# Turning attention outputs by two half-height row groups of TensorE: a sliding-window attention and mixture-of-experts kernel

## The chip, the cores and the metric

The kernel runs on one core of a Trainium2 chip as one program. The metric is the device time of one execution in microseconds (us), lower is better; a run's time is compared with the kernel before on the same chip. Engines are named as in the profile: PE is TensorE (PEld its weight loads), DVE is VectorE, ACT is ScalarE, POOL is GpSimd, SP issues transfers.

## The reference

Attention with a window of 64 positions runs over 8 batches of 8 heads, 576 positions and 64 values each. Its output, laid out as 4608 tokens by 512 values, is x. Each token goes to the one of 8 experts with the largest logit, and its result is scaled by that expert's softmax weight.

```python
rel = pos[:, None] - pos[None, :]
mask = (rel >= 0) & (rel < window)
scores = np.where(mask, scores, -1000000000.0)
scores = scores - np.max(scores, axis=-1, keepdims=True)
attn = np.exp(scores)
attn = attn / (np.sum(attn, axis=-1, keepdims=True) + 1e-09)
x = (attn @ v).transpose(0, 2, 1, 3).reshape(B * S, H * D)
logits = x @ w_gate
expert_idx = np.argmax(logits, axis=1)
probs = np.exp(logits - logits.max(-1, keepdims=True))
probs /= probs.sum(-1, keepdims=True) + 1e-09
gate_w = probs[np.arange(N), expert_idx]
y = np.maximum(x_e @ w1[e], 0.0) @ w2[e]        # for the tokens of each expert e
out = gate_w[:, None] * y
```

## The kernel before, in words

The program has two parts. In the first, attention and routing run in one software pipeline of 48 steps; in the second, the tokens of each expert are gathered and go through the two expert products. The change touches the first part alone.

A unit is two batches (a batch group) and two heads, and there are 16 units, four to a batch group. A unit has three steps; a step handles three tiles of 128 query positions for both heads. The function step (L1089) writes out, for a step s, what each engine does in order, and every engine runs its own list in that order:

- scored(s + 1) (L743): 24 products of q and k into banks 0 and 1 of PSUM, one bank per head; masked(s + 1) (L756) on DVE adds the mask and takes the row minimum; softened (L766) on ACT takes the exponentials.
- weighted(s - 1) (L791): 24 products with v into bank 6.
- logits (L846), in the third step of a unit only: 18 products with the gate's weights for the unit before; L851 or L853 on DVE adds them up.
- flipped(s) (L775): 12 transposes of the exponentials, each over 64 partitions, six into one bank and six into another. L778 copies the first bank to SBUF on DVE (pT, first half) and the second on ACT (second half).
- divided(s - 1) (L801, L802, L805) on DVE reads bank 6 and writes x into the tile xs.
- turned(s + 3): transposes of q and k, L707 (16 of 64 partitions, two banks, two copies L713 on ACT) or, in the third step of a unit, L698 (two of 128 partitions, one bank, copy L701).
- x_turned(s - 2) (L818): three transposes of x over 128 partitions into one bank, and the copy L821 on ACT into a tile xT, which the logits read later.

The banks of flipped, turned, x_turned and logits come from one ring, tr_ring (L594): banks 2, 3, 4, 5 and 7 in turn. A use of a bank waits until the use five places earlier has been copied out. From step 41 on the ring has four banks (L1139).

Three names for steps are used below. x_turned(s - 2) handles the third of a unit's three parts in a **middle step** (s mod 3 = 1), the first part in a **closing step** (s mod 3 = 2, the one with the logits and L698), and the second part in a **pair step** (s mod 3 = 0).

Of the kernel before, what the change touches and what calls it, by code (L numbers as in the profile page):

```python
# [11 lines left out]
F32 = mybir.dt.float32  # L12
# [24 lines left out]
def kernel(  # L37
# [10 lines left out]
    nc = tc.nc  # L48
    P = nc.NUM_PARTITIONS
    B, H, S, D = q.shape  # L50
# [39 lines left out]
    ident = consts.tile([P, P], F32, name="ident")  # L90
# [38 lines left out]
    banks = [Memory(banks_p.tile([P, 512], F32, name=f"bank{i}")) for i in range(8)]  # L129
# [54 lines left out]
    with tc.tile_pool(name="tmp", bufs=1) as tmp:  # L184
# [8 lines left out]
        for i in range(BG):  # L193
# [14 lines left out]
            out=behind[:], in_=behind[:], pattern=[[-1, P]], compare_op=ALU.is_ge, fill=0.0, base=0,  # L208
# [44 lines left out]
    ST = 3  # L253
    NST = NTB // ST
# [331 lines left out]
    with tc.manual_schedule(), ExitStack() as brief, ExitStack() as held:  # L586
# [2 lines left out]
        rp = held.enter_context(tc.tile_pool(name="rp", bufs=2))  # L589
        att = brief.enter_context(tc.tile_pool(name="att", bufs=2))  # L590
        sd = brief.enter_context(tc.tile_pool(name="sd", bufs=3))
        xp = brief.enter_context(tc.tile_pool(name="xp", bufs=3))
        lt = brief.enter_context(tc.tile_pool(name="lt", bufs=1))
        sc_ring, tr_ring = cycle((0, 1)), cycle((2, 3, 4, 5, 7))  # L594

# [6 lines left out]
            out=half[:, n : n + 1], in_=half[:, n : n + 1], fill=MASKED, pattern=[[0, 1], [rest[0], P]],  # L602
# [16 lines left out]
        units = [(bg, g) for bg in range(B // BG) for g in range(NG)]  # L619
        NU = len(units)  # L620

        halves = (slice(0, D), slice(D, P))
        qks, sides, rests, Ts, xss, xTs, lgs, logits_of = {}, {}, {}, {}, {}, {}, {}, {}
# [185 lines left out]

        last = B // BG - 1  # L810

        def x_turned(s):
            u, c = divmod(s, NST)
            bg, g = units[u]
            xTs[s] = xp.tile([P, ST * P], F32, name="xT")
            tr = banks[next(tr_ring)](0, ST, P)
            for m in range(ST):
                nc.tensor.transpose(  # L818
                    out=tr[:, m, :], in_=xss[bg, c][:, m, g * P : (g + 1) * P], identity=ident[:]
                )  # L820
            nc.scalar.copy(out=xTs[s][:], in_=tr.rearrange("p m s -> p (m s)"))  # L821
# [267 lines left out]
        def step(s):  # L1089
# [30 lines left out]
            if 0 <= s - 2 < N:  # L1120
                x_turned(s - 2)
# [15 lines left out]
        for s in range(-3, N):  # L1137
            if s == N - NST * NG + NST + 2:
                tr_ring = cycle((2, 3, 4, 5))  # L1139
# [6 lines left out]
        tr_ring = cycle((4, 5))  # L1146
# [6 lines left out]
        for c in (1, 2):  # L1153
            store(last, c, nc.sync)
        x_turned(N - 2)
        sums_x(tps)
        gather_first(perm_e[:, C : 2 * C])
        by_tok = [by_tokens(last, c) for c in range(NST)]
        next(by_tok[0])
        next(tile0)  # L1160
        logit(N - 2)
        x_turned(N - 1)
        next(by_tok[0], None)
        next(by_tok[1])
# [167 lines left out]
```

## Time and profile before

| | |
|---|---|
| median of 3 runs | 688.19 us (686.51 to 688.44) |
| the profiled execution's own time | 684.57 us |
| its span | 682.8 us |
| PE busy over the span | 656.1 us (96%) |
| ACT busy over the span | 284.3 us (42%) |
| DVE busy over the span | 494.2 us (72%) |

The span runs from the first to the last instruction that the profiler saw. A row of the timeline has the start, the busy length, the engine, the line, the operation and what it writes and reads, and how many instructions were merged into it; in square brackets stands how long the engine was idle before and what released it. Matmuls overlap, so a group's busy length reaches into the next group's: what a group costs PE is the time from its start to the next group's start.

### The profile page before, as it was taken

What the parts mean: (1) busy time and instruction counts of PE and PEld (TensorE: products, weight loads), DVE (VectorE), ACT (ScalarE), POOL (GpSimd) and SP (SyncE); (2) the same over time, 40 slices, a digit from 0 to 9 for tenths busy, and PEclk for the clock granted to TensorE, in tenths of its full rate; (3) what the DMA queues carried; (4) which work ended last, traced back from release to release, by engine and by line L of the source; (5) the groups of instructions that cost most, each with busy time, mean ns of one, the idle gap of its engine ahead of it and who ended that gap; (6) DMA issues with size and microseconds to landing.
All of it is one profiled execution on the core that took longest, in us unless ns stands there. A gap on an engine that the chain in (4) does not pass through costs nothing. (4 is left out here: it accounts for less than half of the span.)

```text
span 682.8 us, 18995 instructions
## 1 busy us (share of the span) xinstructions
PE 656.1 (96%) x7385; PEld 571.5 (84%) x7385; DVE 494.2 (72%) x1598; ACT 284.3 (42%) x699; POOL 354.5 (52%) x407
## 2 busy tenths in 40 slices
PE   7799999999889999999999999999999999999996
PEld 4678878787779987988999999899699789699995
DVE  5678998998839666856686676577775786866864
ACT  5779898999833222212222212212331222232220
POOL 7556777573171337578451546546285566264112
PEclk9999999999999999999999999999999999999999
DMA  9999979684360461725501280270254171212021
GB/s 205 233 268 305 208 197 275 172 245 135 129 203 6 146 227 55 248 64 172 191 12 54 65 276 34 79 265 32 67 191 161 47 270 46 65 41 65 4 62 63
DMA packets 94657, 95.22 MB, mean 139 GB/s; under 512 B 58063, under 2 KB 73439, under 8 KB 94528
## 3 DMA queue, kind: packets, MB, share of 16 engines
q1 hardware_dynamic: 72000, 34.58, 19.8%
q10 hardware_dynamic: 13920, 32.05, 13.7%
q0 software_dynamic: 8608, 26.88, 12.5%
q8 instruction: 80, 1.31, 0.8%
q14 instruction: 49, 0.40, 0.2%
HBM read 74.32 MB, written 20.74 MB: 139 GB/s over the span
## 5 line engine op out<-in xcount | busy, mean ns | idle before, releaser
L337 DVE STREAM_TRANSPOSE v_m<-xg 32x256 f32<-32x256 f32 x320 | 139.3, 435 | 19.5 <-ACT xg L322 13.4
L293 POOL DMA_INDIRECT xg<-x_dram,at_g x42 | 44.5, 1059 | 171.7 <-ACT qk_m L349 122.5
L366 PE MATMUL bank<-qk_m,s 128*128 128x128 f32 x1024 | 122.5, 275 | 0.0
L366 PEld LDWEIGHTS bank<-qk_m,s 128*128 128x128 f32 x1024 | 118.3, 192 | 0.1
L766 ACT ACTIVATE pr<-pr,mx 128x128 f32<-128x128 f32 x288 | 89.7, 396 | 12.9 <-DVE mx L756 12.7
L366 PE MATMUL bank<-qk_m,w 128*128 128x128 f32 x768 | 94.1, 276 | 0.6 <-PEq L1236 0.6
L366 PEld LDWEIGHTS bank<-qk_m,w 128*128 128x128 f32 x768 | 90.4, 192 | 4.0 <-issue 3.6
L756 DVE CUSTOM_DVE_ANT_0 pr<-bank,mask 128x128 f32<-128x128 f32 x288 | 64.5, 285 | 19.7 <-PE bank L743 18.2
L408 DVE TENSOR_TENSOR v_m<-bank,v_m 128x256 f32<-128x256 f32 (+1 forms) x95 | 43.9, 480 | 35.5 <-PE bank L412 26.6
L312 POOL DMA_INDIRECT out_dram<-v_m,at_s x42 | 42.6, 1013 | 50.8 <-DVE v_m L408 46.9
L791 PEld LDWEIGHTS bank<-v_m,pT 128*64 128x64 f32 x1152 | 40.6, 139 | 14.6 <-DVE xs L805 9.6
L146 POOL TENSOR_TENSOR s<-w 128x1024 f32<-128x1024 f32 x22 | 52.2, 2375 | 0.0
L791 PE MATMUL bank<-v_m,pT 128*64 128x65 f32 x1152 | 47.3, 229 | 4.6 <-DVE xs L805 2.7
L412 PE MATMUL bank<-qkT_m,v_m 128*128 128x256 f32 x216 | 48.1, 379 | 0.0
L679 POOL COPY v_m<-v_m 64x520 f32<-64x520 f32 x32 | 20.1, 628 | 51.8 <-DMA v_m<-in_v_dram 41.3
L349 ACT COPY qk_m<-v_m 128x512 f32<-128x512 f32 x40 | 22.7, 615 | 57.0 <-DVE v_m L337 57.0
L412 PEld LDWEIGHTS bank<-qkT_m,v_m 128*128 128x128 f32 x216 | 41.0, 190 | 5.6
L373 ACT COPY qk_m<-bank 128x512 f32<-128x512 f32 x16 | 9.4, 586 | 86.3 <-PE bank L366 66.4
L743 PE MATMUL bank<-qkT_m 64*64 64x128 f32 x1152 | 44.2, 282 | 0.4 <-DVE mx L756 0.3
L378 DVE TENSOR_TENSOR qk_m<-bank,qk_m 128x512 f32<-128x512 f32 x16 | 11.1, 692 | 38.4 <-PE bank L366 24.1
L743 PEld LDWEIGHTS bank<-qkT_m 64*64 64x64 f32 x1152 | 32.1, 134 | 8.0 <-issue 3.4
L412 PE MATMUL bank<-s,v_m 128*128 128x256 f32 x168 | 37.4, 379 | 0.0
(212 smaller groups left out, 1234.7 us busy)
## 6 DMA issues: line engine op xcount, KB each, us to landing
w<-in_moe_w_dram ACTq DMA_DIRECT2D x11, 2048.0 KB, 8.2
qk_m<-in_q_dram SPq DMA_DIRECT2D x32, 256.0 KB, 5.0
v_m<-in_v_dram SPq DMA_DIRECT2D x64, 128.0 KB, 4.6
qk_m<-in_k_dram SPq DMA_DIRECT2D x30, 256.0 KB, 5.1
qk_m<-in_moe_w_dram ACTq DMA_DIRECT2D x3, 2048.0 KB, 10.7
w<-in_moe_w_dram ACTq DMA_DIRECT2D x4, 512.0 KB, 5.6
x_dram<-xs POOLq DMA_DIRECT2D x4, 512.0 KB, 4.9
x_dram<-xs SPq DMA_DIRECT2D x4, 512.0 KB, 5.4
```

The source lines that it names most:

```text
L146: op()
L293: G.indirect_dma_start(out=xg_all[:, c], out_offset=None, in_=x_dram[:, :], in_offset=bass.IndirectOffsetOnAxis(ap=at_g[:, c : c + 1], axi ...
L312: put = G.indirect_dma_start(out=out[:, :], out_offset=bass.IndirectOffsetOnAxis(ap=at_s[:, c : c + 1], axis=0), in_=ys[c], in_offset=None ...
L337: V.transpose(out=xn[b * QD : (b + 1) * QD, :, :, a * QD : (a + 1) * QD], in_=rows[a * QD : (a + 1) * QD, :, :, b, :],)
L349: nc.scalar.copy(out=xq[:, :, c], in_=xn[:, c])
L366: nc.tensor.matmul(acc[:, f, :], lhsT=a[:, g, f * P : (f + 1) * P], rhs=b[:, g, :], start=(first and f == 0 and g == 0), stop=(g == HG - 1 ...
L408: plus = lambda out, a, b: V.tensor_tensor(out=out, in0=a, in1=b, op=ALU.add)
L412: nc.tensor.matmul(acc, lhsT=a[:, f, :], rhs=b[:, f, :], start=(start and f == 0), stop=(stop and f == HF - 1), skip_group_check=True,)
L743: nc.tensor.matmul(out_, lhsT=qT[rows, t, a * WINDOW : (a + 1) * WINDOW], rhs=rhs, start=True, stop=True, skip_group_check=True,)
L756: V.tensor_tensor_reduce(out=prs[h][:, m, :], in0=scs[h][:, m, :], in1=mask[:, m0 + m, :], scale=-scale, scalar=-2 * MASKED, op0=ALU.add, ...
L766: nc.scalar.activation(out=y, in_=y, func=AF.Exp, scale=-1.0, bias=mx[:, h, m : m + 1])
L791: nc.tensor.matmul(px[a * D : (a + 1) * D, h, m, :], lhsT=pTs[a][:, h, m, :], rhs=vt[:, h, :], start=True, stop=True, skip_group_check=True,)
```

## The change

The x of the first two parts of a unit is turned together, in the pair step, for all units but the last; the closing step turns no x. Each 128x128 transpose is replaced by two of 64 partitions, one over partitions 0 to 63 and one over 64 to 127, which write to two banks. Twelve such transposes stand where three of 128 partitions stood, and two copies on ACT, one per bank, each 128x384 in pieces of 64, stand where one stood. The third part is turned as before. The xT tiles are split into a pool of two and a pool of one double tile.

```diff
-        xp = brief.enter_context(tc.tile_pool(name="xp", bufs=3))
+        xp = brief.enter_context(tc.tile_pool(name="xp", bufs=2))
+        xp2 = brief.enter_context(tc.tile_pool(name="xp2", bufs=1))
...
+        def x_pair(u):
+
+            bg, g = units[u]
+            xT = xp2.tile([P, 2, ST, P], F32, name="xT2")
+            trs = [banks[next(tr_ring)](0, 2, ST, D) for _ in range(2)]
+            for c in range(2):
+                xTs[u * NST + c] = xT[:, c].rearrange("p m s -> p (m s)")
+                for m in range(ST):
+                    for tr, r in zip(trs, halves):
+                        nc.tensor.transpose(
+                            out=tr[:, c, m, :], in_=xss[bg, c][r, m, g * P : (g + 1) * P], identity=ident[r, r]
+                        )
+            for tr, r in zip(trs, halves):
+                nc.scalar.copy(
+                    out=xT.rearrange("p c m s -> p (c m) s")[:, :, r], in_=tr.rearrange("p c m s -> p (c m) s")
+                )
+
         def x_turned(s):
             u, c = divmod(s, NST)
             bg, g = units[u]
+            if u < NU - 1 and c < 2:
+                if c == 1:
+                    x_pair(u)
+                return
             xTs[s] = xp.tile([P, ST * P], F32, name="xT")
```

In the changed kernel the line numbers shift: L743, L775, L707 and L698 become L744, L776, L708 and L699, the transposes of x_pair are L822, and the matmuls of the routing at L901 become L923. In the rows below bank_81 to bank_88 are banks 0 to 7, in order, and a name such as side_1914 is one buffer of the tile side. DVE_49 and Activation_49 stand for a semaphore that the engine raises.

The first place is PE's list in a pair step of the middle of the program, from flipped to the next scored. Before:

```order
L775 MATMUL bank_84<-ident,pr_1848 128x64
L775 MATMUL bank_85<-ident,pr_1848 128x64
...
L707 MATMUL bank_86<-ident,side_1821 128x64 [waits Activation_49,Pool_49]
L707 MATMUL bank_88<-ident,side_1821 128x64 [waits Activation_49]
...
L818 MATMUL bank_83<-ident,xs 128x128 [waits Activation_49]
L818 MATMUL bank_83<-ident,xs 128x128 x2
L743 MATMUL bank_81<-qkT_m 64x128 [waits DVE_49]
```

And in the changed kernel:

```order
L776 MATMUL bank_83<-ident,pr_1876 128x64
L776 MATMUL bank_84<-ident,pr_1876 128x64
...
L708 MATMUL bank_85<-ident,side_1849 128x64 [waits Pool_49]
L708 MATMUL bank_86<-ident,side_1849 128x64 [waits Activation_49]
...
L822 MATMUL bank_88<-ident,xs 128x64 [waits Activation_49]
L822 MATMUL bank_83<-ident,xs 128x64 [waits DVE_49]
...
L744 MATMUL bank_81<-qkT_m 64x128
```

The step took five banks of the ring and now takes six, so the second bank of x_pair (83) is the one that flipped wrote first in the same step, and its transposes wait for DVE, whose L778 copies that bank out.

The second place is PE's list in step 41, a closing step, where the ring has just become four banks long; L901 is the routing's product of an earlier batch group. Before:

```order
L775 MATMUL bank_83<-ident,pr_3978 128x64
L775 MATMUL bank_84<-ident,pr_3978 128x64
...
L698 MATMUL bank_85<-ident,qk_m 128x128 x2
L818 MATMUL bank_86<-ident,xs 128x128 x3
L901 LDWEIGHTS behind [waits DVE_49]
L901 MATMUL bank_83<-oh_all,behind 128x72 [waits Activation_49]
L743 MATMUL bank_81<-qkT_m 64x128 [waits DVE_49]
```

And in the changed kernel:

```order
L776 MATMUL bank_83<-ident,pr_4046 128x64
L776 MATMUL bank_84<-ident,pr_4046 128x64
...
L699 MATMUL bank_85<-ident,qk_m 128x128 x2
L923 LDWEIGHTS behind
L923 MATMUL bank_86<-oh_all,behind 128x72 [waits DVE_49]
L744 MATMUL bank_81<-qkT_m 64x128 [waits DVE_49]
```

The three transposes of x are gone from the closing step, as in every closing step up to step 44, and L923 has the fourth bank (86) where it had the first (83), so it no longer waits for ACT.

The third place is PE's list in the next step, 42, a pair step with four banks. Before:

```order
L707 MATMUL bank_86<-ident,side_4048 128x64 [waits Activation_49,Pool_49]
L707 MATMUL bank_83<-ident,side_4048 128x64 [waits Activation_49]
...
L818 MATMUL bank_84<-ident,xs 128x128 [waits DVE_49]
L818 MATMUL bank_84<-ident,xs 128x128 x2
L743 MATMUL bank_81<-qkT_m 64x128
```

And in the changed kernel:

```order
L708 MATMUL bank_85<-ident,side_4116 128x64 [waits Activation_49,Pool_49]
L708 MATMUL bank_86<-ident,side_4116 128x64 [waits Activation_49]
...
L822 MATMUL bank_83<-ident,xs 128x64 [waits DVE_49]
L822 MATMUL bank_84<-ident,xs 128x64 [waits Activation_49]
...
L744 MATMUL bank_81<-qkT_m 64x128
```

Here the first bank of x_pair waits for DVE's copy of the same step, as the one bank did before, and the second waits for ACT's.

## Rows read from the trace of the kernel before

**Rows 1.** Timeline of PE over one unit, closing step to closing step (us).
```profile
100.98 0.59 PE L775 MATMUL bank<-ident,pr 64*128 64x64 f32 x12
101.50 0.44 PE L698 MATMUL bank<-ident,qk_m 128*128 128x128 f32 x2
101.78 0.49 PE L818 MATMUL bank<-ident,xs 128*128 128x128 f32 x3
102.20 0.89 PE L743 MATMUL bank<-qkT_m 64*64 64x128 f32 x24
103.18 0.97 PE L791 MATMUL bank<-v_m,pT 128*64 128x65 f32 x24
104.08 0.58 PE L775 MATMUL bank<-ident,pr 64*128 64x64 f32 x12
104.50 0.67 PE L707 MATMUL bank<-ident,side 64*128 64x64 f32 x16
105.10 0.55 PE L818 MATMUL bank<-ident,xs 128*128 128x128 f32 x3
105.57 0.89 PE L743 MATMUL bank<-qkT_m 64*64 64x128 f32 x24
...
109.60 0.97 PE L791 MATMUL bank<-v_m,pT 128*64 128x65 f32 x24
...
111.29 0.58 PE L775 MATMUL bank<-ident,pr 64*128 64x64 f32 x12
```

**Rows 2.** The same unit, DVE.
```profile
101.11 0.55 DVE L853 TENSOR_TENSOR lgT<-bank,lgT 96x384 f32<-96x384 f32 x1 [0.33 <-PE bank L846]
...
102.56 0.56 DVE L805 TENSOR_TENSOR xs<-bank,rec 128x384 f32<-128x384 f32 x1
104.69 0.56 DVE L778 COPY pT<-bank 128x384 f32<-128x384 f32 x1 [0.21 <-PE bank L775]
```

**Rows 3.** The same unit, ACT.
```profile
106.61 0.48 ACT L821 COPY xT<-bank 128x384 f32<-128x384 f32 x1
106.98 1.88 ACT L766 ACTIVATE pr<-pr,mx 128x128 f32<-128x128 f32 x6
108.75 0.48 ACT L778 COPY pT<-bank 128x384 f32<-128x384 f32 x1
```

**Rows 4.** Waits of PE from 20 to 195 us: total, times, longest.
```profile
PE bank L707 <- POOL side L652: 4.1, 3, 2.5
PE bank L791 <- DVE xs L805: 2.7, 9, 0.5
```

**Rows 5.** Timeline of PE and ACT in two units with routing work.
```profile
88.70 0.97 PE L791 MATMUL bank<-v_m,pT 128*64 128x65 f32 x24 [0.47 <-DVE xs L805]
98.76 0.47 ACT L778 COPY pT<-bank 128x384 f32<-128x384 f32 x1
99.13 1.07 PE L791 MATMUL bank<-v_m,pT 128*64 128x65 f32 x24
```

**Rows 6.** Timeline of steps 41 and 42, PE, DVE and ACT.
```profile
167.54 0.20 PE L901 MATMUL bank<-oh_all,behind 128*128 128x72 bf16 x1 [0.49 <-ACT pT L778]
167.71 0.89 PE L743 MATMUL bank<-qkT_m 64*64 64x128 f32 x24
168.65 0.29 DVE L756 CUSTOM_DVE_ANT_0 pr<-bank,mask 128x128 f32<-128x128 f32 x1 [1.21 <-PE bank L743]
170.73 0.55 PE L818 MATMUL bank<-ident,xs 128*128 128x128 f32 x3 [0.21 <-DVE pT L778]
170.81 0.46 ACT L778 COPY pT<-bank 128x384 f32<-128x384 f32 x1
171.21 0.89 PE L743 MATMUL bank<-qkT_m 64*64 64x128 f32 x24
```

**Rows 7.** Timeline of step 44, a closing step, and what follows it.
```profile
179.36 0.89 PE L743 MATMUL bank<-qkT_m 64*64 64x128 f32 x24
180.40 0.29 DVE L756 CUSTOM_DVE_ANT_0 pr<-bank,mask 128x128 f32<-128x128 f32 x1 [0.53 <-PE bank L743]
```

## The prediction

> **What bounds the kernel now.** I read the page first (PE busy in nearly every slice), then PE's timeline over one undisturbed unit, DVE's and ACT's beside it, the table of waits, and last the steps in which PE stands still. The change lives in the first 190 us; the expert part behind it has the same instructions and simply starts earlier or later.
>
> In the undisturbed unit [rows 1] PE is hardly ever idle: from 104.08 to 111.29 each group starts when the one before is through. A unit takes 111.29 - 100.98 = 10.31 us. One stop is left, in the closing step. There L791 starts at 103.18 because bank 6 is being read by L805 on DVE until 102.56 + 0.56 = 103.12 [rows 2]; the release takes 0.06. DVE itself is late because its list goes L853, L778, L801, L802, L805, and L853 waits for PE's logits [rows 2]. So a closing step is a chain from the logits on PE through DVE back to PE, and x is no part of it. PE waits for L805 nine times in the table [rows 4].
>
> **Prices.** On PE, from start to start [rows 1]:
> - twelve transposes of 64 partitions, followed by another such group: 104.08 to 104.50, 0.42;
> - twelve followed by a group of another shape: 100.98 to 101.50, 0.52; so a change of shape costs 0.10;
> - sixteen and a change: 104.50 to 105.10, 0.60; without the change 0.50;
> - three of 128 partitions and a change: 0.42 in the closing step, 0.47 in the pair step; without the change 0.32.
>
> **Closing step: x removed.** L743 starts 0.32 earlier, at 101.88. L791 behind it still starts at 103.18, for L805 is unmoved: DVE's list hangs on the logits, which come before. L756 follows L805 on DVE and is unmoved too. Gain on the path: nothing, hidden by L805. ACT does one copy less, 0.37 from start to start (106.61 to 106.98 is one copy's share [rows 3]); its exponentials then wait for L756 anyway.
>
> **Pair step: x of two parts.** Without any wait, sixteen of L707 with no change of shape behind them (0.50) and twelve of x_pair with one (0.52) are 1.02, where 104.50 to 105.57 was 1.07: L743 would start 0.05 earlier. But the order shows that the second bank of x_pair is the bank that flipped wrote first in the same step, and waits for L778 on DVE. That copy runs from 104.69 to 105.25 [rows 2], since it waits for the twelve transposes of flipped itself; with 0.06 for the release the second transpose starts at 105.31. The first one has gone ahead at 105.00 and gains nothing: PE's list is served in order, so the other ten, L743, L791, and in time the logits stand behind the blocked one. From 105.31 the pairs and the change of shape take 0.47 to 0.52 (the twelve's price, with or without its first pair): L743 at 105.78 to 105.83, against 105.57. I take +0.2, near the lower one.
>
> Nothing takes this back before the closing step, since PE has no gap up to 111.29; logits, L853 and L805 move by 0.2, and so does the next unit. The 0.32 saved there is hidden as above. An undisturbed unit becomes 10.31 + 0.2 = 10.51.
>
> ACT now does two x copies in the pair step, so its exponentials start at 107.35 instead of 106.98 and the copy of pT behind them ends at 108.75 + 0.48 + 0.37 = 109.60 [rows 3]. L791 needs it at 109.60 [rows 1], and with PE 0.2 late at 109.80: covered, by PE's own delay alone. If that cover were gone it would cost about 0.06 here. In a unit where it is thin already the whole 0.37 counts: L791 at 99.13 reads pT, whose copy ends at 98.76 + 0.47 = 99.23 [rows 5]. Writing in pieces of 64 instead of a whole row is not in the trace; the copy is bounded by 0.37, its share, and 0.48, its full length, and I take 0.37, the price of the row that it replaces.
>
> The single double tile xT2 costs nothing: the logits that read it run in the closing step before the next pair step. No transfer is added or moved on SP's or POOL's queue.
>
> [...] Here the step goes from five banks of a five-bank ring to six, and rows of this trace show what a ring too short costs: in step 42, with four banks, L818 stood 0.21 for DVE's copy of the same step [rows 6].
>
> **The last steps, with four banks.** In step 41 L901 loses its wait of 0.49 for ACT [rows 6] (another bank), and with 0.32 of x gone L743 starts some 0.8 earlier; L756 has waited 1.21 for it, so DVE follows, and ACT as far as its own list lets it, about 0.6 with one copy less. In step 42 x_pair's second bank waits for ACT's copy of pT, which ended at 170.81 + 0.46 = 171.27; 0.6 earlier plus 0.06 and 0.47 gives L743 at 171.20, where it was 171.21. So PE gives its gain back there, while DVE and ACT keep theirs: between 0 and -0.6, I take -0.3. In step 44, a closing step, L805 does not bind; L756 waited 0.53 for L743 [rows 7], so the 0.32 of x is a real gain, -0.3. In step 45 nothing of q and k is turned and the banks are free; the same chain runs on to the gather that opens the second part.
>
> **Sum.** There are 15 pairs. The first two fall before PE's stops for POOL's sorted q and k (4.1 us in three stops [rows 4]), which swallow 0.2: 0. One falls in a unit whose middle step waits 0.47 for DVE's routing work before L791 at 88.70 [rows 5]: 0. Ten stand in units like the one above: nine at 0.2 and the one at 99.13 with 0.4 make +2.2. The last two: -0.6. Together +1.6: 684.57 becomes 686.2 in the profiled execution (span 682.8 and some 1.8 around it). That execution is 3.6 below the median of the runs, 688.19; the difference put on the median gives 689.8.
>
> **Rivals.**
> 1. The saved PE time reaches the end, because DVE's copies come early enough or the chain through L805 yields. Then a unit saves 0.05 + 0.32 = 0.37, twelve units 4.4, with the tail 5.0: 683.2. For it: PE is busy throughout. Against: L791 at 103.18 ends on L805 to within the release time, and in the pair step the copy ends 0.25 after the first transpose is free to go. [...]
> 2. ACT becomes the bound, place: exponentials and pT of the middle step, price 0.37 a unit, decisive where the copy of pT ends less than 0.37 before L791 needs it. Twelve units 4.4, less 0.6: +3.8, 692.0. For it: the unit at 99.13. Against: in the undisturbed unit PE is late by more than ACT lags, and the closing step gives ACT its copy back.
> 3. The wait is there, but routing work on DVE or ACT hides it in most units, as at 88.70: ten units at 0 to 0.1, with the tail -0.6 to +0.4: about 688. That the halves are not turned together at all would change little by itself: the first half then goes ahead alone, which is what the wait makes of the first pair.
>
> **How the numbers follow.** Forecast 0.52, rival 1 0.15, rival 2 0.13, rival 3 0.20. About 0.3%, or 2.1 us, is what a measurement of this kernel tells from no change. The forecast's own range, 0.1 to 0.3 a unit and the tail between 0 and -0.9, is 688.3 to 691.2; it is on the slower side of the bound four times in ten. Slower: 0.20 of the forecast, 0.12 of rival 2 and 0.01 of rival 3, 0.33. Faster: 0.13 of rival 1 and 0.01 of rival 3, 0.14. Same: 0.53. The range takes in rival 3 and reaches to rival 2 and towards rival 1: 685.6 to 692.2.
>
> **What would show it.** In an undisturbed pair step the transposes of x_pair should show a stop of some 0.3 ended by DVE's pT, and L743 should start 1.27 after the start of the q and k transposes instead of 1.07; in the closing step L743 should be earlier and L791 not, with a longer stop for L805; the unit should be 10.5. Step 41's L923 should show no stop. A unit of 10.0 would make the closing step's reasoning wrong, one of 10.7 the cover of ACT.

## The result: slower, and most of it behind the attention

The changed kernel takes 695.75 us (693.72 to 696.22) against 687.7 of the kernel before; the ratio is 1.0113, with a 95% interval of 1.0087 to 1.0139. I had forecast 689.8 with a range up to 692.2. The profiled execution has a span of 694.5 us against 682.8.

The attention does nearly what was predicted. PE's timeline over an undisturbed ("clean") unit (start, duration, operation, and in brackets the idle time before it with what ended it); it answers to [rows 1]:

```profile
102.55 0.59 PE L776 MATMUL bank<-ident,pr 64*128 64x64 f32 x12
...
103.44 0.89 PE L744 MATMUL bank<-qkT_m 64*64 64x128 f32 x24
104.75 0.97 PE L792 MATMUL bank<-v_m,pT 128*64 128x65 f32 x24 [0.42 <-DVE xs L806]
105.65 0.59 PE L776 MATMUL bank<-ident,pr 64*128 64x64 f32 x12
106.07 0.67 PE L708 MATMUL bank<-ident,side 64*128 64x64 f32 x16
106.58 0.22 PE L822 MATMUL bank<-ident,xs 64*128 64x64 f32 x1
106.95 0.59 PE L822 MATMUL bank<-ident,xs 64*128 64x64 f32 x11 [0.15 <-DVE pT L779]
107.47 0.89 PE L744 MATMUL bank<-qkT_m 64*64 64x128 f32 x24
...
113.18 0.52 PE L776 MATMUL bank<-ident,pr 64*128 64x64 f32 x10
```

One transpose of x_pair goes ahead at 106.58, the other eleven wait for DVE's copy of pT until 106.95, and the closing step's saved time ends in a stop of 0.42 for L806 (the lines have moved by one: L805 is L806, L778 is L779). The unit takes 113.18 - 102.55 = 10.63 instead of 10.31. DVE's copy, which answers to the last of [rows 2], and PE's waits from 20 to 197 us (total, times, longest), which answer to [rows 4]:

```profile
106.34 0.56 DVE L779 COPY pT<-bank 128x384 f32<-128x384 f32 x1 [0.39 <-ACT pr L767]
```

```profile
PE bank L792 <- DVE xs L806: 6.7, 17, 0.7
...
PE bank L822 <- DVE pT L779: 2.9, 13, 0.7
...
PEld bank L792 <- ACT pT L779: 0.4, 2, 0.2
```

At the last L791 of the attention the changed kernel is 2.1 us behind, at 200 us 5.3, and it stays at 4.9 to 5.3 until 590 us. Then comes something that the prediction does not have. PE's timeline in the expert part of the changed kernel, and the same matmuls in the kernel before:

```profile
594.92 0.63 PE L519 MATMUL bank<-w,qk_m 128*32 128x256 f32 x6
598.54 5.85 PE L519 MATMUL bank<-w,qk_m 128*32 128x256 f32 x36 [2.99 <-issue]
```

```profile
589.96 5.52 PE L519 MATMUL bank<-w,qk_m 128*32 128x256 f32 x48
```

Six of 48 equal matmuls run, then PE stands 2.99 us with nothing in the profile to wait for ("issue"). Behind the stop its granted clock is 0.50, as the stretch 599.70 to 602.90 shows (length, PE busy, granted clock, DMA share, GB/s):

```profile
599.70:602.90 3.20, 3.20 (x16) 0.50 0.01 3
```

A second such stop follows at 662 us, in PE's waits from 195 us on (the profile before has neither):

```profile
PE bank L519 <- issue: 3.0, 1, 3.0
PE bank L366 <- issue: 0.7, 1, 0.7
```

By the start times of the same matmuls in both traces the first stop and its half clock cost 5.2 us, the second 1.0.

### The profile page after: what moved, and what is told of

It reads as the page before. It is cut to its first block, busy times and chain, and to the rows that moved or that the text cites. A ratio compares the mean times of both kernels' runs of the same rounds, so it can differ in the third digit from the quotient of the medians.

```text
span 694.5 us, 19208 instructions
## 1 busy us (share of the span) xinstructions
PE 656.3 (95%) x7475; PEld 569.9 (82%) x7475; DVE 492.9 (71%) x1598; ACT 284.4 (41%) x699; POOL 354.0 (51%) x407
## 3 DMA queue, kind: packets, MB, share of 16 engines
q8 instruction: 82, 1.34, 0.8%
## 5 line engine op out<-in xcount | busy, mean ns | idle before, releaser
L366 PE MATMUL bank<-qk_m,w 128*128 128x128 f32 x768 | 95.7, 279 | 1.3 <-issue 0.7
L366 PEld LDWEIGHTS bank<-qk_m,w 128*128 128x128 f32 x768 | 92.1, 195 | 4.6 <-issue 4.2
L792 PEld LDWEIGHTS bank<-v_m,pT 128*64 128x64 f32 x1152 | 40.4, 137 | 17.6 <-DVE xs L806 12.2
L792 PE MATMUL bank<-v_m,pT 128*64 128x65 f32 x1152 | 47.1, 228 | 7.5 <-DVE xs L806 6.7
L744 PE MATMUL bank<-qkT_m 64*64 64x128 f32 x1152 | 43.4, 281 | 0.0
L355 DVE TENSOR_TENSOR qk_m<-v_m,qk_m 128x256 f32<-128x256 f32 x60 | 23.7, 423 | 21.0 <-ACT qk_m L349 20.3
```

The costliest lines, as they stand in the source:

```text
L355: V.tensor_tensor(out=xs[:, n], in0=a, in1=b, op=ALU.subtract)
L366: nc.tensor.matmul(acc[:, f, :], lhsT=a[:, g, f * P : (f + 1) * P], rhs=b[:, g, :], start=(first and f == 0 and g == 0), stop=(g == HG - 1 ...
L744: nc.tensor.matmul(out_, lhsT=qT[rows, t, a * WINDOW : (a + 1) * WINDOW], rhs=rhs, start=True, stop=True, skip_group_check=True,)
L792: nc.tensor.matmul(px[a * D : (a + 1) * D, h, m, :], lhsT=pTs[a][:, h, m, :], rhs=vt[:, h, :], start=True, stop=True, skip_group_check=True,)
```

## The experiments

Both stops follow a jump of PE's program. PE's compiled program has 23,418 instructions before and 23,597 after, 179 more: ninety more transposes, each with its weight load (both pages count as many loads as matmuls: 7,385 before, 7,475 after), less one wait. The queue table of the changed kernel shows code arriving in packets of 1.34 MB / 82 = 16 KiB:

```profile
q8 instruction: 82, 1.34, 0.8%
```

From 20 to 195 us of that trace 29 of these packets start, while PE carries out 3,730 matmuls and 3,726 weight loads, 257 to a packet; in the kernel before, from 20 to 190 us, it is 28 with 3,616 and 3,612, 258. From that I estimate a packet at 256 instructions, taking the queue for PE's alone; such a packet is called a block below.

So the theory, called the code theory below: the change pushes the experts' code against the blocks in which it is fetched, and a jump that lands on a block's last instructions must wait for two blocks. The rival: the stop comes from the later arrival of the work, from more code as such, or from chance. Small matmuls at the start, where PE waits for its first data anyway (0.22, 1.09 and 1.87 us for transfers in the first 12 us of the kernel before), move the code: each is two instructions, a weight load and a matmul. They stand behind the ten 128x512 matmuls with which the program starts (L1053), called the warm-up: in the kernel before nine of them take 0.61 to 0.63 us and the tenth 0.45. A shift below is the number of instructions by which the experts' code lies later than in the kernel before.

**Moved by whole blocks, or by the change's amount.** All by this edit, with K = 39 in the changed kernel and 90 and 128 in the kernel before:

```
+        for _ in range(K):
+            nc.tensor.matmul(
+                banks[7](0, P), lhsT=lo[:, 0], rhs=lo[:, 1], start=True, stop=True, skip_group_check=True,
+            )
```

> The changed kernel with 39 more matmuls (128x128) behind the ten that warm TensorE at the start, where it then waits for the first DMA: 78 more instructions of TensorE, so that with the change's 179 all later code lies 257 instructions, one block of 256 and one more, behind where it lay before. Code theory (the 4.7 us at 595 us come from where the experts' code lies in blocks of 16 KiB): the stop of 3.0 us at the second matmul and the half clock behind it are gone, about 691.0 us (689.8 to 692.5). Rival (the stop follows from the later arrival of the work, or is chance): as the changed kernel, 695.7 +- 1.

> The kernel before with 90 such matmuls, 180 instructions of TensorE, about the shift that the change makes; nothing else is changed. Code theory: attention as before, a stop of about 3 us at the experts' second matmul with half clock behind it, about 692.4 us (690.5 to 693.5). Rival: 687.7 +- 1.

> The kernel before with 128 such matmuls, 256 instructions: one whole block, so that all later code lies in its block as before. Code theory: 687.7 +- 0.7, no stop. A third theory (more matmuls at the start cost by themselves, or more code costs wherever it ends): as the run with 90 or slower, 692 or more. The rival of arrival or chance: 687.7 too.

Ratios to the kernel before, on the same chip: the changed kernel with 39, 1.0050 (1.0032 to 1.0068); the kernel before with 90, 1.0122 (1.0096 to 1.0147); with 128, 1.0012 (0.9998 to 1.0027). Moving its code by 180 instructions alone makes the kernel before as slow as the changed one (695.15 us, above the range expected); by 256 it does not. And the changed kernel gets over half of its loss back from useless work. PE's timeline of the kernel before with 90:

```profile
591.88 0.63 PE L519 MATMUL bank<-w,qk_m 128*32 128x256 f32 x5
594.85 6.71 PE L519 MATMUL bank<-w,qk_m 128*32 128x256 f32 x41 [2.34 <-issue]
```

Five matmuls go ahead here, one fewer than in the changed kernel, for a shift of 180 instead of 179.

**Moved by a few instructions.** The same edit: K = 8 in the changed kernel, 95 and, in a later run, 96 in the kernel before.

> The changed kernel with 8 more matmuls behind the warm-up: 16 instructions of TensorE, so that the code of the experts moves by only 16 more. Code theory, by jumps: in the changed kernel the jump at 591 us lands on the last two instructions of a block of 256, and the jump at 658 us stands 4 instructions behind the start of a block; 16 instructions more put the landing 14 behind the start of the next block and the second jump 20 behind a block's start, so the stop of 3.0 us and its half clock go and the stop at 658 us falls from 0.7 us to 0.4 or less: 691.0 us (690.0 to 692.5). Rival (the more code the worse, or the stop needs a whole block's shift to go): 695.7 +- 1.

> The kernel before with 95 more matmuls, 190 instructions: ten more than in the run with 90, which was 7.8 us slower than before. Code theory, by jumps: the landing at 588 us lies 9 instructions behind a block's start, not on its last: no stop there, and 0.7 us at most at the other jump: 688.0 us (687.2 to 689.5). Rival (more matmuls at the start, or a shift of about 180 to 190 instructions, cost by themselves): 695 as with 90.

The first came as expected: 1.0050 (1.0036 to 1.0065), no stop. The second missed: 1.0126 (1.0109 to 1.0142), 697.2 us. Its trace shows why; PE's matmuls, and its weight loads (PEld):

```profile
602.02 6.78 PE L519 MATMUL bank<-w,qk_m 128*32 128x256 f32 x48 [3.42 <-issue]
```

```profile
598.94 0.11 PEld L519 LDWEIGHTS bank<-w,qk_m 128*32 128x32 f32 x1 [0.74 <-issue]
602.02 0.20 PEld L519 LDWEIGHTS bank<-w,qk_m 128*32 128x32 f32 x7 [2.98 <-issue]
```

One weight load, then the stop. I had taken the program's first instruction for a block's first. The three stops give the edge without that: 12 instructions (six loads, six matmuls) at a shift of 179, 11 at 180, 1 at 190. All sum to 191. The six weight loads of the first two, in the changed kernel and in the kernel before with 90:

```profile
594.92 0.15 PEld L519 LDWEIGHTS bank<-w,qk_m 128*32 128x32 f32 x6 [0.37 <-issue]
```

```profile
591.88 0.15 PEld L519 LDWEIGHTS bank<-w,qk_m 128*32 128x32 f32 x6 [0.43 <-issue]
```

> The kernel before with 96 more matmuls, 192 instructions, one matmul more than the run that took 697.2 us. Code theory, with the block's edge where the three stops put it: after the jump at 588 to 595 us TensorE did 12 instructions before it stopped at a shift of 179, 11 at 180 and 1 at 190, so the edge lies at a shift of 191. At 192 the landing is the second instruction of a block: no stop there, and the 0.7 us at the next jump stay: 688.6 us (687.4 to 690.0). Rival (the matmuls at the start, or the amount of code, cost by themselves): 697 +- 1, as with 95.

The run with 96 gave 1.0017 (1.0000 to 1.0034), 690.05 us: one matmul more at the start, and the kernel is 1.1% faster, each run measured against the kernel before on its own chip. All 48 matmuls run through, as they do in the changed kernel with 8:

```profile
594.77 5.52 PE L519 MATMUL bank<-w,qk_m 128*32 128x256 f32 x48 [0.23 <-issue]
```

The jumps themselves stand in the profile as instructions of PE's queue; durations in ns, least, median and most, for the jump ahead of the first stop, L1271 in the changed kernel and L1249 in the kernel before:

```profile
L1271 PEldq COMPARE_BRANCH  x1: 3685/3685/3685, 591.2 to 591.2; - x1
```

```profile
L1249 PEldq COMPARE_BRANCH  x1: 3677/3677/3677, 586.2 to 586.2; - x1
```

Of the 43 jumps in each of the two traces most take 0.04 to 0.4 us, one in the changed kernel takes 1.6, and the long ones, eight before and seven after, 3.3 to 4.7; each of these fifteen ends 1.3 to 1.6 us after a packet of the instruction queue has landed. In the kernel before PE has no stop for "issue" behind the long jumps of the expert part: matmuls already issued cover them (the one above ends at 589.9, the matmuls issued ahead of it at 590.0). So the jump alone is not the first stop: it takes the same 3.7 us in both.

The packets of the instruction queue show what comes on top. In the changed kernel one of 16 KiB lands at 593.46 us, 1.4 us before that jump ends, and another at 597.02, 1.5 us before PE goes on. In the kernel before the second lands at 591.48, while PE is at work. The second stop of the changed kernel, at 662 us, is the end of a jump of 4.5 us (L1259) that the matmuls ahead of it did not cover. So a long jump took 3.3 to 4.7 us here, and where the block's edge lay 1 to 12 instructions behind the landing PE stood another 2.3 to 3.4 us (2.34 with 90, 2.99 in the changed kernel, 3.42 with 95).

**What the attention loses.** First the pair step without row groups, six full transposes into the same two banks:

```
+            trs = [banks[next(tr_ring)](0, ST, P) for _ in range(2)]
...
-                    for tr, r in zip(trs, halves):
...
+                    nc.tensor.transpose(
+                        out=tr[:, m, :], in_=xss[bg, c][:, m, g * P : (g + 1) * P], identity=ident[:]
+                    )
...
```

> The changed kernel, but x of both steps is turned in the pair step by six transposes of 128 partitions, three into each of the two banks, with a copy for each step: the move to one step and the wait stay, the row groups go, and TensorE has one instruction less than before the change. Wait theory: the second bank is free 0.88 us after the turn of q and k starts (as in the changed kernel), three transposes of 0.107 us follow, so the next scores start 1.30 us after that point, against 1.40 with row groups and 1.07 before: a clean unit 10.5 us, +1.5 to +2.5 us at the end of attention, the row groups having earned nothing. Rival (row groups shorten the path): clean unit 10.75 or more. Code theory: no stop in the experts, so in all 689.5 to 692.5 (the lower end if the 3.2 us at the transition come from the code too, the upper if they come from the delay). Arrival theory: the stop comes here as well, 694 or more.

1.0019 (1.0004 to 1.0035), 688.4 us, under the 689.5 to 692.5 expected, and no stop in the experts. PE, same step as above:

```profile
106.30 0.67 PE L708 MATMUL bank<-ident,side 64*128 64x64 f32 x16
106.90 0.87 PE L821 MATMUL bank<-ident,xs 128*128 128x128 f32 x6
107.71 0.89 PE L744 MATMUL bank<-qkT_m 64*64 64x128 f32 x24
```

From L708 to L744 it takes 1.41 us, against 1.40 with row groups, and the unit is 10.62. I had expected 1.30; there is no wait in it, the six simply follow each other. So row groups win nothing at this place: what they save, the wait takes. The whole is even 0.3% shorter without them than with them and 39 matmuls (1.0019 against 1.0050), with the same clean unit; in the two profiled executions 0.8 us of that lie in the attention, and where the rest comes from is not shown.

Then the pair with its wait taken away, by turning it one step later behind the next scores (with 8 matmuls at the start):

```
-                if c == 1:
-                    x_pair(u)
...
-                prs[s + 1] = softened(*masked(s + 1, scored(s + 1)))
+                scs = scored(s + 1)
+                if s >= NST + 1 and s % NST == 1:
+                    x_pair((s - NST) // NST)
+                prs[s + 1] = softened(*masked(s + 1, scs))
```

> The changed kernel with 8 more matmuls as in the run beside it, and x of the pair turned one step later, behind the next scores instead of ahead of them: the first bank that flipped wrote has been copied long before, so no wait. Wait theory: in the pair step the next scores start 0.6 us after the turn of q and k begins instead of 1.40, and the twelve transposes (0.42 us and 0.10 for the change of mode) stand between those scores and the weighted sum: a clean unit 10.35 to 10.5 us against 10.63, and 1.5 to 4 us less than the run beside it. Rival (ScalarE, whose two copies of x come half a microsecond later and push the exponentials behind them, takes the wait's place): a clean unit 10.6 or more, no gain.

The clean unit fell to 10.35, as the wait theory has it. PE, pair step and the step behind it:

```profile
51.13 0.67 PE L708 MATMUL bank<-ident,side 64*128 64x64 f32 x16
51.73 0.89 PE L744 MATMUL bank<-qkT_m 64*64 64x128 f32 x24
52.55 0.59 PE L822 MATMUL bank<-ident,xs 64*128 64x64 f32 x12
53.07 0.97 PE L792 MATMUL bank<-v_m,pT 128*64 128x65 f32 x24
```

The whole gained only 0.8 us on the changed kernel with 8, where 1.5 to 4 were expected: 1.0027 (1.0015 to 1.0039) against 1.0050; in the profiled execution the last unit was 1.8 us longer, and two stops for "issue" cost 2.3.

Then row groups for the second step's x alone, the first's left where it stood (52 matmuls at the start; x_groups does for one step what x_pair does for two):

```
-            if u < NU - 1 and c < 2:
-                if c == 1:
-                    x_pair(u)
+            if u < NU - 1 and c == 1:
+                x_groups(u, c)
                 return
...
```

> x of the unit's first step stays in the closing step with three full transposes, as before the change; only x of the second step is turned by two row groups, six half transposes into two banks, in the pair step. 52 more matmuls at the start put the code of the experts where the run with 8 has it. Wait theory: the second bank is free 0.88 us after the turn of q and k starts, and 0.21 us of transposes and 0.10 follow: the next scores start 1.19 us after that point (before 1.07, changed kernel 1.40), a clean unit 10.43 us, about +2 us over before in all, two thirds of the pair step's loss being the x of the other step that was moved into it. Rival (each use of row groups, or a sixth use of the five banks, costs the 0.3 us whatever it turns): a clean unit 10.6.

The clean unit is 10.37: of the 0.32 that the change costs, 0.26 is gone when the closing step's x stays where it was. The whole did not follow: 1.0062 (1.0049 to 1.0075), some 4 us where 2 were expected. In the profiled execution the attention lost 1.9 us on the mean of the kernel before, about as much as the changed kernel; 0.9 of it is one stop for "issue" before L792. I cannot say where the rest of the 4 us went.

**Other pairings.** If the fault is that covered work was paired with uncovered, the second and third step should be paired.

```
-            if u < NU - 1 and c < 2:
-                if c == 1:
+            if u < NU - 1 and c > 0:
+                if c == 2:
                     x_pair(u)
...
```

> The changed kernel, but x of the unit's second and third step is turned together by row groups, at the place in the middle step where the third's x stood, and x of the first step stays in the closing step as before the change; 13 more matmuls at the start keep the experts' code off the block's edge. If the loss of the change was that it moved covered work (the closing step's x) into a step that is not covered: the pair step loses its x (0.47 us), the middle step gains 0.33 us, a clean unit 10.17 us (before 10.31, changed kernel 10.63), and about 686.5 us (685.0 to 688.5). Rival (row groups or the wait for the bank cost as much here): a clean unit 10.3 to 10.6, 688 to 691.

A miss: the clean unit 10.43, the whole 1.0041 (1.0022 to 1.0060). PE:

```profile
107.27 0.67 PE L708 MATMUL bank<-ident,side 64*128 64x64 f32 x16
107.87 0.89 PE L744 MATMUL bank<-qkT_m 64*64 64x128 f32 x24
108.97 0.97 PE L792 MATMUL bank<-v_m,pT 128*64 128x65 f32 x24 [0.21 <-DVE xs L806]
...
110.29 0.67 PE L708 MATMUL bank<-ident,side 64*128 64x64 f32 x16
110.80 0.22 PE L822 MATMUL bank<-ident,xs 64*128 64x64 f32 x1
111.17 0.58 PE L822 MATMUL bank<-ident,xs 64*128 64x64 f32 x11 [0.15 <-DVE pT L779]
111.69 0.89 PE L744 MATMUL bank<-qkT_m 64*64 64x128 f32 x24
```

The two PE intervals are as worked out (0.60 and 1.40), but with the pair step shorter L792 now waits for L806 there. The chain through DVE was close behind. And the unit that starts with step 41 took 14.17 us, against 12.09 in the changed kernel.

The same pair behind the closing step's scores, the logits moved behind flipped:

```
+                scs = scored(s + 1)
+            if s >= NST + 2 and s % NST == 2:
+                x_pair((s - NST) // NST)
...
-            ripe = 0 <= s - 3 < N and s % NST == NST - 1 and logits((s - 3) // NST)
             if 0 <= s < N:
                 pTs[s] = flipped(s, prs.pop(s))
...
+            ripe = 0 <= s - 3 < N and s % NST == NST - 1 and logits((s - 3) // NST)
```

> As the run beside it, but the pair (second and third step) is turned in the closing step, behind the scores and ahead of the weighted sum, and the logits are moved behind the turn of the probabilities in that step. No wait for a bank: pair and middle step lose their x (0.47 us each), the closing step gains 0.52 us: a clean unit 9.9 us, and with what other units keep of it 684.5 us (682.5 to 687.5), faster than both kernels. Rival (the logits, in the same step as their x now, wait for ScalarE's copies, or ScalarE's copies hold up its exponentials): a clean unit 10.3 or more, 687.5 to 692.

The clean unit is 9.99, the shortest of all; the whole is 0.9993 (0.9970 to 1.0016): no difference that can be told. With the last two pairs (those of steps 44 and 47) turned singly:

> As the late pair of the second and third step, but the last two pairs that it had (units 13 and 14), which waited 1.1 and 0.4 us for ScalarE's copies in a ring of four banks, are turned step by step as before the change; 20 more matmuls at the start keep the experts' code off the block's edge. Theory: the clean unit stays 9.99 us, unit 13 falls from 12.05 to about 10.9 us, and the whole is 1 to 1.5 us less than with the late pair in all units: 0.4 to 0.5% faster than the kernel before (ratio 0.995 to 0.997). Rival (what the late pair wins in the units is lost elsewhere, in waits that follow): a ratio of 0.998 or more.

1.0005 (0.9984 to 1.0026): the gain did not come. But the run does not test what was expected of it. The wait of 1.1 us stands in step 41, the last step of unit 13, where the pair that is turned is the x of unit 12, and the edit left that pair in place; unit 13 stayed at 12.04 us with the same stop in it:

```profile
168.33 0.27 PE L822 MATMUL bank<-ident,xs 64*128 64x64 f32 x1 [0.86 <-ACT qkT_m L714]
```

Only the wait of 0.4 us, in step 44, was taken out, and the unit from step 41 did not gain by it (12.00 us against 11.58). Whether the four banks cause the longer wait stays untested. No version here is shown to be faster than the kernel before.

## Why the prediction was wrong, step by step

**"The expert part behind it has the same instructions and simply starts earlier or later": this step failed.** The instructions are the same, but they lie elsewhere in the program. It cost 1.1% in the kernel before (1.0126 with 95 matmuls against 1.0017 with 96; 1.0122 with 90 against 1.0012 with 128), and 0.6% of the changed kernel's 1.1% (1.0113 against 1.0050, both with 39 and with 8). No rival had it. Without it the kernel would have been at about 691, inside the range.

**Closing step, right.** L744 comes earlier and L792 does not, with 0.42 of idle time for L806 in place of the 0.32 and the old margin of 0.10. That the x moved had been free there is shown by the run that left it there (10.37).

**Pair step, right in kind, too small.** The wait is where it was named, but L744 starts 1.40 after L708, not 1.27: the copy starts 0.69 after flipped instead of 0.61 [rows 1, 2], and from its end to L744 it is 0.57 instead of 0.53. I had chosen the lower end. The profile puts DVE's wait before it down to ACT's exponentials, but with six full transposes the copy comes as late (106.57, 0.69 after flipped) where the same wait is put down to PE; so why it starts later stays open. The unit became 10.63, not 10.51.

**Sum over the attention.** From the closing step that starts near 47 us to the last L791 five profiled executions with the code before take 143.4 to 144.5 us (mean 144.1), three with the changed code 145.7 to 146.3 (mean 146.1): +2.0 where +1.6 was forecast. Of that, +2.4 lie ahead of flipped in step 41, where +2.2 was forecast, and -0.4 behind it, where -0.6 was. The sum came out near though a clean unit lost 0.32 and not 0.2, so other units lost less than it has them lose; executions of the same code differ by up to 1.9 us there, so how near is in part luck.

**The last steps, right.** L923 starts without a stop. In step 42 the second bank of x_pair stood for ACT, and PE gave back there what it had gained, as forecast. Before, flipped of step 41 and the scores behind step 45:

```profile
165.77 0.59 PE L775 MATMUL bank<-ident,pr 64*128 64x64 f32 x12
...
182.07 0.89 PE L743 MATMUL bank<-qkT_m 64*64 64x128 f32 x24
```

And in the changed kernel:

```profile
168.17 0.58 PE L776 MATMUL bank<-ident,pr 64*128 64x64 f32 x12
...
168.95 0.20 PE L923 MATMUL bank<-oh_all,behind 128*128 128x72 bf16 x1
...
172.52 0.27 PE L822 MATMUL bank<-ident,xs 64*128 64x64 f32 x1 [0.21 <-DVE pT L779]
173.15 0.58 PE L822 MATMUL bank<-ident,xs 64*128 64x64 f32 x11 [0.36 <-ACT pT L779]
173.66 0.89 PE L744 MATMUL bank<-qkT_m 64*64 64x128 f32 x24
...
184.13 0.89 PE L744 MATMUL bank<-qkT_m 64*64 64x128 f32 x24
```

The changed kernel is 2.40 us late at flipped of step 41, 2.45 at the scores behind step 42 (171.21 before [rows 6]) and 2.06 behind step 45. The stretch from that flipped to those last scores takes 16.3 us in each of the five executions with the code before and 15.97, 15.58 and 15.59 with the changed code: 0.6 less on average, the forecast's own -0.6.

**ScalarE, right.** PE's weight loads wait for its copy of pT 0.4 us in all, in two places (the last row of the waits above), so rival 2 did not happen; nor did 1 and 3.

**The profiled execution as a base.** Between 190 and 200 us the profiled execution after lost another 3 us, half of it at a granted clock of 0.50, which it had for 6.7 us where the one before had it for 3.4:

```profile
196.80:203.50 6.70, 5.84 (x29) 0.50 0.40 128
```

```profile
192.90:196.30 3.40, 3.07 (x17) 0.51 1.01 356
```

I first took this for an effect of the change. But the kernel before has the long stretch as well, with 90 matmuls at the start, and with 128 it has none:

```profile
193.40:199.90 6.50, 6.36 (x31) 0.50 0.61 207
```

```profile
190.00:200.00 10.00, 7.26 (x82) 1.00 0.79 264
```

PE stands still before it, waiting for gathered rows (L328 for xg, 1.9 us before and 3.6 after), and executions differ. It belongs to neither kernel, and it is part of why the two profiles lie 11.7 us apart and the medians 8. Of the 0.5% that the changed kernel keeps with its code back in place, 0.3% is the attention; the kernel before with 128 and 96 matmuls at the start lies at 0.1 to 0.2% itself, so little is left to explain.

## What to carry to other kernels

Count the instructions that a change adds ahead of a jump: they move all code behind them, and here a landing on the last 1 to 12 instructions of a block cost 0.6 to 1.1% of the time, in a part that nobody touched. Before judging a change of some 1%, add or drop a few harmless instructions and measure again. And work that is paired to run side by side must come from places that both count: here half of it had been covered, and the bank that the pair needed made the other half wait for its whole gain.

## What the runs showed that I had not expected

- One 128x128 matmul at the start, almost six hundred microseconds ahead, changed the time by 1.1%, and the stop moved by exactly as many instructions as the code.
- The stop of 2.99 us cost more than itself: behind it the granted clock was 0.50 for at least 3.2 us, by my estimate from these two figures another 1.6 us of work.
- Straight code stopped too. In the run with the late pair PE stood 0.77 us in the middle of twelve equal transposes with nothing to wait for:

```profile
62.90 0.40 PE L822 MATMUL bank<-ident,xs 64*128 64x64 f32 x6
64.06 0.40 PE L822 MATMUL bank<-ident,xs 64*128 64x64 f32 x6 [0.77 <-issue]
```

  The run with the tail turned singly shows 2.0 us of the same before a group of L776. What PE waited for in either was not shown.
- A clean unit is a poor measure of the whole: with 0.32 us less in each (9.99 against 10.31) the attention of the profiled execution was 2.4 us shorter (141.6 against 144.1 on average), and the runs cannot tell the whole from the kernel before.
